# Routing of a token-choice mixture: compare and one-hot matrices by token column, idle products moved behind the first choice

## The chip, the cores and the metric

The kernel runs as one launch on one NeuronCore of a Trainium2 chip. The metric is the device time of that core in microseconds (us), the median of three runs. A core has a tensor engine (PE in the profile; its weight loads, the loads of the stationary operand, are listed apart as PEld), a vector engine (DVE), a scalar engine (ACT), a general engine (POOL) and a queue that issues transfers (SP). Each engine works through its own instructions in the order in which they were issued; engines wait for each other through semaphores.

## What is computed

Three layers, one after the other: attention with a compressive memory, a dense layer with a rational activation, and a mixture of experts. The change touches the last alone. Of the reference, cut:

```python
def _moe2_ref(x, w_gate, w1, w2):            # N = 2304 tokens, D = 512, E = 8 experts, F = 1024
    cap = N // E                             # 288
    order = np.argsort(-(x @ w_gate).flatten())
    for idx in order:
        tok, e = (int(idx) // E, int(idx) % E)
        if assigned[tok] >= 0 or counts[e] >= cap:
            continue
        assigned[tok] = e
        counts[e] += 1
...
    for e in range(E):
        mask = assigned == e
        out[mask] = np.maximum(x[mask] @ w1[e], 0.0) @ w2[e]
```

All pairs of token and expert are visited from the largest logit to the smallest; a pair is taken if the token is free and the expert has fewer than 288 tokens.

## The kernel before

**Two programs in a row.** `main` computes attention, the dense layer and the logits of all tokens (to about 869 us); `route` assigns the tokens and computes the experts (from there to the end). Nothing of `main` is changed.

**A choice.** `route` never sorts. In eight rounds (`phase(p)`, called a choice here) it finds which expert fills up next and which 288 tokens it gets. The logits lie as `Lt`, 128 partitions by 18 token columns by 8 experts. In a choice every free token stands for its best expert (`E1`, a one-hot over 8); the largest logit threshold at which some expert has 288 candidates is searched as an integer key of three digits, each by two passes of `search` (`st` = 45, then 1), so six passes. The last choice searches nothing. A pass is a ring between two engines:

- DVE compares 45 thresholds with each token's digit: `cm`, 810 elements of float16 on 128 partitions, laid out as 45 rows (thresholds) of 18 token columns;
- PE counts: 18 products, one for each token column c, whose stationary matrix is `cm[:, :, c]` (128 by 45; neighbours lie 18 elements, 36 bytes, apart) and whose moving matrix is `E1[:, c]` (8 columns), summed into `cnt` in PSUM;
- DVE flags what reaches 288 (`fl`) and sums the flags; PE adds them over the thresholds onto all partitions with one product by `one`; DVE takes `st` times that sum from the digit (`r`). After every second pass three small DVE operations (`dh`, `da`, `r`) bring in the next digit.

Behind the passes a choice computes the expert's number `ei`, the members (`GE`, counted by products with `one` and `tri`), their positions (`pos`), and turns positions to token numbers: `OH`, a one-hot over 32 (576 elements as 32 rows of 18 columns), is the stationary operand of 18 more products with `pay`; their sum is copied (`pls`) and made into three lists of 96 token numbers (`ids`, `id`).

**An expert.** `gather` fetches the 288 rows by three indirect transfers that POOL issues (`yg`), `px` transposes them on PE, ACT and DVE split them into two float16 parts (`x`). `prep` loads the expert's weights (`rawa`, `rawb`; 4 MB together), which ACT and DVE split into `hia`, `loa`, `hib`, `lob`. `ffn` then multiplies: 96 products into `ph`, 96 into `po`, each with 288 moving columns, for the last expert 288 with 96. ACT and DVE empty `ph` (`hh`, `hl`); `send` transposes back and scatters rows to `out`.

**The order.** No instruction order is written by hand. Every operation is recorded, and `plan` makes a list schedule: an engine takes the operation of smallest priority number (`S.now`) among those that are ready by its table of costs. Choices are recorded at -1.0, expert p at about p, so the choices of later experts are drawn in between the products of earlier ones. The instructions are then issued in that order on every engine; all of them carry line 408 in the profile, and groups are told apart by tile names. Where `plan` sees PE wait ahead of the first product into a fresh float32 bank (`o.fresh`), it puts idle products of `idh` (128 columns, into the same place, read by nobody) in front; they are meant to keep the tensor engine's clock up.

Of the kernel before, what the change touches and what calls it, by code (L numbers as in the profile page):

```python
# [27 lines left out]
CAP = N // E  # L28
NC_ = N // 128
XS = 1024.0          # scale of x before its split  # L30
WS = 256.0           # scale of w_in, w_out before their split
DS = 1024.0          # scale of dg and of the gate's deviations
# [8 lines left out]
class View:  # L41
    """a tile or a part of one, made in the program when it is used"""
# [43 lines left out]
    def region(self):  # L86
        """the partitions and the bytes in them that the view covers"""
        if self.a is None:
            return 0, 1 << 30, 0, 1 << 30
        pb = self.t.pbytes  # L90
        o = self.a.__array_interface__["data"][0] - DUMMY.ctypes.data
        p, lo = divmod(o, pb)
        ends = [s * (n - 1) for s, n in zip(self.a.strides[1:], self.a.shape[1:])]
        hi = lo + self.a.itemsize + sum(x for x in ends if x > 0)
        return p, p + self.a.shape[0], lo + sum(x for x in ends if x < 0), hi


class Late:
    """an operand made when it is used, from parts of tiles and the result of an operation"""
# [8 lines left out]
class LTile(View):  # L108
# [9 lines left out]
    def reset(self, S):  # L118
        """a tile that an earlier schedule made"""
# [11 lines left out]
class Group:  # L131
    """tiles of equal room that the schedule hands out to whoever needs one first"""
# [42 lines left out]
class Sched:  # L175
# [16 lines left out]
    def record(self, eng, name, args, kw):  # L192
# [25 lines left out]
        o.fresh = None          # room in its bank that nothing has been written to  # L218
        if eng == "tensor" and w[0].t.dt == F32:
# [19 lines left out]
        if eng == "tensor":             # the groups of a bank one after the other  # L239
# [17 lines left out]
    def plan(self):  # L257
        """start times by a list schedule: an engine takes the first of its operations that are ready"""
# [10 lines left out]
        hold = {}          # operations that wait for a tile's slot or a pool  # L269
# [8 lines left out]
        def grant(tag, t):  # L278
            """the tag's next tiles take the slots that are free"""
# [28 lines left out]
        while done < len(ops):  # L308
# [37 lines left out]
            if e == "tensor":           # its clock is halved after a window of little work  # L346
# [3 lines left out]
                if o.fresh is not None:  # L350
                    # while it waits, products to the same place that nobody reads keep the clock up
# [16 lines left out]
            if o.lat < 0:           # a transfer: the queue is free, the data come later  # L368
                dma[0] = max(dma[0], end + (0.65 if o.name != "dma_start_transpose" else 0.1)) - o.lat
                fin = dma[0] + 0.9  # L370
                if o.name == "indirect_dma_start" and o.kw["in_offset"] is None:     # the next waits for it
# [52 lines left out]
SLACK = 1.6, 1.3     # for the two schedules  # L424
HW, HN = 3.41333, 3050     # the window of the tensor engine's clock, and the columns that keep it fast
# [11 lines left out]
def cost(o, w, r):  # L437
    """what the operation holds its engine for, in us"""
# [70 lines left out]
def main(S, q, k, v, M_prev, z_prev, beta, w_in, w_out, moe_a, moe_b, w_gate):  # L509
# [25 lines left out]
    # identity and index constants  # L535
# [21 lines left out]
    # the attention of the later batches beside the blocks of tokens that are ready  # L557
# [16 lines left out]
GB = [None]          # banks of PSUM  # L574
LIM = dict(s=3, loc=2, y=2, m=4)    # how many a kind may hold
TS = 3.2
TAIL = 6             # first block of the MLP with no attention beside it
# [3 lines left out]
EARLY = 4            # units of attention that run before the MLP  # L581
# [3 lines left out]
L1E = 0.0            # the same for the last block  # L585
GA = 0.3             # how much more urgent the gate of the last but one tokens is
# [5 lines left out]
XR = 2, 2            # parts of x kept  # L592
# [6 lines left out]
U_ATT = 14           # steps of a unit of attention  # L599
MS = 8               # steps of a block of the MLP  # L600


def merge(S, streams):
    """draw n steps from each stream, spread over its span; a stream's lead makes it more urgent"""
# [16 lines left out]
def params(nc, consts, beta, moe_a, moe_b):  # L621
    """the small parameters, broadcast to every partition"""
# [7 lines left out]
    # exp(-beta) - 1 from t = -beta / 64: a short series, then m -> m (m + 2) six times  # L630
# [21 lines left out]
    # the numerator of dg = g - g0, by DS: h (a1 + (a2 - g0 |b1|) h + a3 h^2) - g0 |b0| |h|  # L652
# [13 lines left out]
def attention(nc, ac, wk, ps, xb, X, G0, P0, q, k, v, M_prev, z_prev):  # L666
# [6 lines left out]
    # causal masks of the diagonal blocks, added by the tensor engine  # L673
# [9 lines left out]
    # tiles whose padding is set once  # L683
    V1, PH, MZ, QR = [], [], [], []
    for i in range(2):
# [4 lines left out]
        t = ac.tile([128, 2, 130], F16, name=f"mz_{i}")         # the memory, split, and beside it zeros  # L690
# [3 lines left out]
    # the parts of a unit, in chunks of 128 tokens: the last 64 on partitions 64.. of the last chunk  # L694
# [13 lines left out]
    def phi(p, c0, c1):  # L708
        """PS (elu(q) + 1), split"""
# [11 lines left out]
    def split(p, n, w):  # L721
        """AS p in two parts"""
# [5 lines left out]
    def turn(a, w, how):  # L728
        """AS a in two parts, with the keys on partitions"""
        t = wk.tile([128, 1024], F16, name="at", bufs=TB)  # L730
        a = a[:, 0:w]
        if how == 3:        # by the tensor engine
# [8 lines left out]
        if how == 2:        # the lower part on GpSimd  # L741
# [12 lines left out]
    def qk(u):  # L754
# [22 lines left out]
        # q and k with features on partitions, split  # L777
        g = wk.tile([128, 4, S], F16, name="qkg", bufs=1)       # high parts of q and k, low parts of k and q
# [16 lines left out]
        # for a head: q over its low parts, k likewise, and k with the parts swapped  # L795
# [9 lines left out]
    def memory(u):  # L805
        """the part of the memory, with its norm"""
# [980 lines left out]
```

## Time and profile before

| | us |
|---|---|
| median of 3 runs | 1239.42 (1238.64 to 1240.16) |
| span of the profiled execution | 1236.9 |
| busy in it: PE / DVE / ACT / POOL | 1020.0 / 1006.7 / 690.1 / 629.6 |
| first compare products of the first choice | at 872.2 |
| first products of the first expert | at 909.9 |
| last products of the last expert (`po`) | from 1228.49 |

The profile is one execution, recorded instruction by instruction. A "busy" column is the time in which an engine ran at least one instruction; a row `x18` in a timeline merges 18 instructions that follow each other. For a tile's rows three durations are given, min/median/max in ns. `PEclk` is the granted clock of the tensor engine as a share of 2.4 GHz; its other level, 1.2 GHz, is 0.50. An entry `[0.20 <-DVE E]` is idle time of the engine ahead of the row, and what ended it.

### The profile page before, as it was taken

The page shows a single profiled execution, that of the slowest core. Times are in us where ns is not written, and L with a number is a line of the kernel's source. Part 1 is how long each engine was busy: PE and PEld are TensorE (multiplying, and loading weights), DVE is VectorE, ACT ScalarE, POOL GpSimd, SP SyncE. Part 2 cuts the span into 40 slices and gives each one's busy share as a digit, 9 for nine tenths or more (in the row PEclk, how much of TensorE's full clock was granted, in tenths as well). Part 3 has the DMA queues.
Part 4 walks back from the last instruction along what each step waited for, and adds up shares of the span by engine and source line. Part 5 has one row for each costly group of instructions (what it writes and reads, how often), then busy time and mean ns, then how long its engine had stood idle before and what let it go on. Part 6 is the DMA issues. An engine that isn't in the chain of part 4 may idle for free. (4 is left out here: it accounts for less than half of the span.)

```text
span 1236.9 us, 28684 instructions
## 1 busy us (share of the span) xinstructions
PE 1020.0 (82%) x11140; PEld 751.2 (61%) x11140; DVE 1006.7 (81%) x2309; ACT 690.1 (56%) x1443; POOL 629.6 (51%) x549
## 2 busy tenths in 40 slices
PE   4567877777788887887988989985789989999997
PEld 3445544354455655565665766663677767777776
DVE  7999999999999898999898989898466655766531
ACT  5776766546666776676775655650044434444542
POOL 3466578885766566656756556562031423334311
PEclk8688888987999998899999999996569988998999
DMA  8766564124565465555454211120044343543521
GB/s 212 211 155 144 114 138 119 22 27 69 138 106 109 96 121 108 106 100 106 86 91 70 53 19 35 32 65 10 1 156 156 108 143 101 175 145 129 165 87 40
DMA packets 220415, 125.77 MB, mean 102 GB/s; under 512 B 190870, under 2 KB 197110, under 8 KB 220152
## 3 DMA queue, kind: packets, MB, share of 16 engines
q1 hardware_dynamic: 217208, 114.51, 39.1%
q0 software_dynamic: 3072, 9.44, 2.6%
q8 instruction: 87, 1.43, 0.5%
q14 instruction: 48, 0.39, 0.1%
HBM read 71.96 MB, written 9.46 MB: 66 GB/s over the span
## 5 line engine op out<-in xcount | busy, mean ns | idle before, releaser
L408 PE MATMUL b<-W2h,dg 128*128 128x512 f16 x576 | 194.7, 393 | 15.2 <-POOL dg L408 8.0
L408 DVE TENSOR_TENSOR_SCAN yd<-A,b 128x256 f32<-128x256 f32 x272 | 165.5, 663 | 10.3 <-PE b L408 10.3
L408 PE MATMUL b<-X,W1h 128*128 128x64 f16 (+3 forms) x2432 | 168.5, 220 | 0.0
L408 POOL TENSOR_TENSOR nm<-nm,dn 128x512 f32<-128x512 f32 x72 | 98.4, 1368 | 95.9 <-ACT dn L408 51.4
L408 PEld LDWEIGHTS <-W1h 128*128 128x128 f16 x2432 | 137.2, 99 | 7.9 <-issue 2.5
L408 PEld LDWEIGHTS <-dg 128*128 128x128 f16 x864 | 80.1, 100 | 96.0 <-issue 16.5
L408 ACT ACTIVATE a<-b,mx 128x512 f32<-128x512 f32 (+4 forms) x160 | 78.5, 521 | 84.9 <-DVE b L408 59.9
L408 POOL TENSOR_TENSOR dn<-dn,u 128x512 f32<-128x512 f32 x72 | 98.8, 1374 | 43.4 <-ACT dn L408 41.7
L408 POOL TENSOR_TENSOR dg<-nm,dg 128x512 f16<-128x512 f32 x72 | 90.6, 1261 | 44.1 <-ACT dg L408 43.9
L408 PE MATMUL b<-W2l,dg 128*128 128x512 f16 x288 | 112.8, 392 | 0.0
L408 ACT ACTIVATE dn<-dn 128x512 f32<-128x512 f32 x144 | 90.1, 628 | 33.3 <-POOL dn L408 32.1
L408 PE MATMUL b<-X,W1l 128*128 128x64 f16 (+3 forms) x1216 | 98.6, 222 | 6.4 <-DVE yd L408 3.3
L408 PE MATMUL b<-qk 128*128 128x128 f16 (+5 forms) x384 | 75.8, 328 | 20.7 <-DVE at L408 9.6
L408 PE MATMUL ph<-x,hia 128*128 128x288 f16 x512 | 88.2, 306 | 0.0
L408 PEld LDWEIGHTS <-W1l 128*128 128x128 f16 x1216 | 73.2, 100 | 19.0 <-issue 6.0
L408 PE MATMUL b<-Wd,gT 99*128 99x64 f16 x1088 | 51.4, 199 | 40.1 <-DVE yd L408 12.0
L408 POOL DMA_INDIRECT yg<-Yd,id x24 | 33.8, 1408 | 97.6 <-ACT hia L408 41.0
L408 PE MATMUL b<-vh,at 128*128 128x65 f16 (+1 forms) x768 | 61.4, 205 | 25.7 <-DVE yd L408 5.2
L408 PEld LDWEIGHTS <-at 128*128 128x128 f16 x1152 | 54.1, 102 | 46.6 <-issue 29.9
L408 PEld LDWEIGHTS <-cm 128*45 128x45 f16 x756 | 68.0, 182 | 22.0 <-DVE E L408 7.6
L408 PEld LDWEIGHTS <-gT 99*128 99x128 f16 x1088 | 44.2, 102 | 60.8 <-DVE yd L408 20.7
L408 DVE TENSOR_SCALAR_CACHE_REDUCE b<-b 128x512 f32<-128x512 f32 (+4 forms) x160 | 75.7, 487 | 6.5 <-PE b L408 5.9
(250 smaller groups left out, 2716.5 us busy)
## 6 DMA issues: line engine op xcount, KB each, us to landing
rawa<-moe_w SPq DMA_DIRECT2D x32, 512.0 KB, 3.8
rawb<-moe_w SPq DMA_DIRECT2D x32, 512.0 KB, 4.0
qk<-qkg SPq DMA_DIRECT2D x64, 216.0 KB, 3.6
raw<-moe_w_in SPq DMA_DIRECT2D x16, 512.0 KB, 4.9
raw<-moe_w_out SPq DMA_DIRECT2D x16, 512.0 KB, 6.6
Yd<-yt SPq DMA_DIRECT2D x17, 256.0 KB, 2.0
qkr<-k SPq DMA_DIRECT2D x32, 128.0 KB, 2.5
qkr<-q SPq DMA_DIRECT2D x32, 128.0 KB, 3.2
```

Source lines behind the costliest of these rows:

```text
L408: o.ins = f(*[real(x) for x in o.args], **{k: real(x) for k, x in o.kw.items()})
```

## The change

- `cm` and `OH` keep their contents but are stored by token column: 18 columns of 45 thresholds, 18 columns of 32 positions. The tables they are compared with (`kst`, `io32`) are laid out alike. A stationary matrix `cm[:, c, :]` or `OH[:, c, :]` is now 45 or 32 neighbouring elements. In the comparison the token's value is repeated along the innermost dimension (step 0), where before it was read along it (step 1).
- The product that sums the flags has a stationary matrix of -45 or -1 (`less`) in place of ones, so that `r` is one addition; two memsets make the matrices, two signs turn in the expert's number.
- `plan` no longer puts idle products in front of `cnt` products (the condition on the name `cnt`).
- In the first choice 12 products of `idh` with 512 columns of `OH` are recorded behind the `OH` products, into a bank of `px`.

The diff without its hunks that only drop comments:

```diff
-        if eng == "tensor" and w[0].t.dt == F32:
+        if eng == "tensor" and w[0].t.dt == F32 and w[0].t.name != "cnt":
             o.fresh = w[0] if w[0].t.wr else w[0].t[:, 0:128]
...
-    kst = {st: iota([128, KT, C], [[st, KT], [0, C]], st if st == 1 else st + 1, 0, f"kst{st}", F16) for st in (KT, 1)}
-    io32 = iota([128, 32, C], [[1, 32], [0, C]], 1, 0, "io32", F16)
+    kst = {st: iota([128, C, KT], [[0, C], [st, KT]], st if st == 1 else st + 1, 0, f"kst{st}", F16) for st in (KT, 1)}
+    io32 = iota([128, C, 32], [[0, C], [1, 32]], 1, 0, "io32", F16)
...
+    less = {}
+    for st in (KT, 1):
+        less[st] = rc.tile([KT, 128], F16, name=f"less{st}")
+        nc.vector.memset(less[st], -float(st))
...
-            cm = rk.tile([128, KT, C], F16, name="cm")
-            nc.vector.tensor_tensor(cm, kst[st], r[:, None, :].to_broadcast([128, KT, C]), OP.is_le)
+            cm = rk.tile([128, C, KT], F16, name="cm")
+            nc.vector.tensor_tensor(cm, kst[st], r[:, :, None].to_broadcast([128, C, KT]), OP.is_le)
...
-                nc.tensor.matmul(pc[0:KT, 0:E], cm[:, :, c], E1[:, c, :], start=c == 0, stop=c == C - 1)
+                nc.tensor.matmul(pc[0:KT, 0:E], cm[:, c, :], E1[:, c, :], start=c == 0, stop=c == C - 1)
...
-            nc.tensor.matmul(pb[:, 0:1 + E], one[0:KT, :], fl, start=True, stop=True)
+            nc.tensor.matmul(pb[:, 0:1 + E], less[st], fl, start=True, stop=True)
...
-            nc.vector.scalar_tensor_tensor(r2, pb[:, 0:1].to_broadcast([128, C]), -float(st), r, op0=OP.mult, op1=OP.add)
+            nc.vector.tensor_scalar(r2, r, pb[:, 0:1], None, op0=OP.add)
...
-            nc.vector.scalar_tensor_tensor(fe, pb[:, 1:1 + E], -16.0, em8, op0=OP.mult, op1=OP.add)
+            nc.vector.scalar_tensor_tensor(fe, pb[:, 1:1 + E], 16.0, em8, op0=OP.mult, op1=OP.add)
...
-            nc.vector.scalar_tensor_tensor(me, pb[:, 0:1], 16.0, mf, op0=OP.mult, op1=OP.add)
+            nc.vector.scalar_tensor_tensor(me, pb[:, 0:1], -16.0, mf, op0=OP.mult, op1=OP.add)
...
-        OH = rk.tile([128, 32, C], F16, name="OH")
-        nc.vector.tensor_tensor(OH, io32, posh[:, None, :].to_broadcast([128, 32, C]), OP.is_equal)
+        OH = rk.tile([128, C, 32], F16, name="OH")
+        nc.vector.tensor_tensor(OH, io32, posh[:, :, None].to_broadcast([128, C, 32]), OP.is_equal)
...
-            nc.tensor.matmul(pl[0:32, 0:18], OH[:, :, c], pay[:, c].rearrange("p a j -> p (a j)"), start=c == 0, stop=c == C - 1)
+            nc.tensor.matmul(pl[0:32, 0:18], OH[:, c, :], pay[:, c].rearrange("p a j -> p (a j)"), start=c == 0, stop=c == C - 1)
+        if p == 0:
+            up = ps.tile([128, 512], F32, name="px", bufs=2)
+            for _ in range(WARM):
+                nc.tensor.matmul(up, G0["idh"], OH.rearrange("p c k -> p (c k)")[:, 0:512], start=True, stop=True)
...
+WARM = 12
```

The change also moves instructions, since `plan` works with other costs. PE, first choice, between the first and the second pass, before (`E_13306` is `E1`; 7 idle products ahead of the flag product, 12 behind it; in the whole program 146 idle products into `cnt`):

```order
L408 LDWEIGHTS cm
L408 MATMUL cnt<-E_13306,cm 45x8
L408 LDWEIGHTS idh
L408 MATMUL cnt<-idh 128x128
...
L408 LDWEIGHTS one
L408 MATMUL cnt<-fl,one 128x9
L408 LDWEIGHTS idh
L408 MATMUL cnt<-idh 128x128
...
L408 LDWEIGHTS cm
L408 MATMUL cnt<-E_13306,cm 45x8
```

The same place now (`less_13269` is the matrix of -45):

```order
L408 LDWEIGHTS cm
L408 MATMUL cnt<-E_13309,cm 45x8
L408 LDWEIGHTS less_13269
L408 MATMUL cnt<-fl,less_13269 128x9
L408 LDWEIGHTS cm
L408 MATMUL cnt<-E_13309,cm 45x8
```

Between the passes of the first choice PE now issues nothing but the ring's own products.

PE at the end of the first choice now; where before 6 idle products into `cnt` stood ahead of the `OH` products and 5 behind, 12 into `px` and 2 of the new 512-column products stand ahead and 10 behind:

```order
L408 MATMUL cnt<-GE,tri 128x36
L408 LDWEIGHTS idh
L408 MATMUL px<-idh 128x128
...
L408 LDWEIGHTS idh
L408 MATMUL px<-OH,idh 128x512
...
L408 LDWEIGHTS OH
L408 MATMUL cnt<-pay,OH 32x18
...
L408 LDWEIGHTS idh
L408 MATMUL px<-OH,idh 128x512
```

The 10 behind stand ahead of the first compare products of the second choice.

DVE behind the first choice, a piece of the difference (`pls` to `id` make the lists that the first gather waits for; `loa` is the low part of a piece of the first expert's weights):

```order
+L408 TENSOR_TENSOR cm<-kst_13256,kf_13602 128x810
 L408 COPY pls<-cnt 32x18
+L408 SCALAR_TENSOR_TENSOR loa<-rawa,hia 128x512
 L408 SCALAR_TENSOR_TENSOR ids<-pls 32x3 x3
-L408 COPY id_13726<-ids 96x1
-L408 COPY id_13729<-ids 96x1
-L408 COPY id_13733<-ids 96x1
+L408 SCALAR_TENSOR_TENSOR loa<-rawa,hia 128x512
+L408 COPY id_13647<-ids 96x1
+L408 COPY id_13649<-ids 96x1
+L408 COPY id_13652<-ids 96x1
```

Two weight pieces that stood behind the three lists now stand between their steps.

## Rows read from the trace of the kernel before

**Rows 1.** The page: the span.

```profile
span 1236.9 us, 28684 instructions
```

**Rows 2.** Busy time by stretch: PE, PEld, DVE, ACT, POOL, then PEclk, DMA.

```profile
900.50:939.20 38.70, 36.70 (x296) 28.67 (x295) 24.25 (x104) 17.66 (x37) 10.67 (x9) 0.74 0.43 150
939.20:978.10 38.90, 38.48 (x321) 30.31 (x321) 23.04 (x99) 18.29 (x38) 13.07 (x12) 0.91 0.42 144
978.10:1021.30 43.20, 38.66 (x315) 30.30 (x314) 26.95 (x102) 17.92 (x39) 12.96 (x12) 0.86 0.34 117
1021.30:1060.00 38.70, 37.76 (x316) 29.34 (x315) 24.33 (x95) 16.46 (x37) 11.53 (x10) 0.89 0.37 120
1060.00:1098.40 38.40, 37.05 (x323) 29.42 (x322) 25.82 (x100) 18.56 (x40) 13.83 (x12) 0.96 0.41 141
1098.40:1142.60 44.20, 41.73 (x353) 32.79 (x353) 27.32 (x111) 20.99 (x46) 16.49 (x15) 0.92 0.41 142
1142.60:1229.00 86.40, 81.76 (x869) 68.71 (x869) 33.35 (x72) 37.01 (x83) 20.97 (x15) 1.00 0.32 107
```

**Rows 3.** DVE's waits, 924 to 1144 us: total, times, longest.

```profile
DVE fl L408 <- PE cnt L408: 48.9, 31, 2.9
DVE r L408 <- PE cnt L408: 19.8, 23, 2.2
```

**Rows 4.** Tile cm: durations in ns, min/median/max.

```profile
L408 PEld LDWEIGHTS <-cm x756: 158/183/186, 872.2 to 1130.6; 128*45 128x45 f16 x189
L408 DVE TENSOR_TENSOR cm<-kst,r x35: 567/582/2795, 875.1 to 1127.9; 128x810 f16<-128x810 f16 x35
```

**Rows 5.** Tile OH: durations in ns.

```profile
L408 PEld LDWEIGHTS <-OH x144: 135/159/163, 898.0 to 1143.6; 128*32 128x32 f16 x144
L408 DVE TENSOR_TENSOR OH<-io,posh x8: 449/450/453, 897.5 to 1141.1; 128x576 f16<-128x576 f16 x8
```

**Rows 6.** A load of neighbouring columns (by form); 16 short products in a row (timeline).

```profile
L408 PEld LDWEIGHTS <-qk 128*64 128x64 f16 x128 | 6.7, 115 | 19.3 <-issue 9.7 <-DVE at L408 6.3 <-DVE yd L408 1.3
...
470.05 0.63 PE L408 MATMUL b<-Wd,gT 99*128 99x64 f16 x16 [0.15 <-DVE qkg L408]
470.51 0.95 PE L408 MATMUL b<-X,W1h 128*128 128x64 f16 x14
```

**Rows 7.** Timeline of the first choice: its start, its third pass, its end.

```profile
872.16 1.71 PE L408 MATMUL cnt<-E,cm 128*45 128x8 f16 x18 [7.40 <-DVE E L408]
...
880.29 1.71 PE L408 MATMUL cnt<-E,cm 128*45 128x8 f16 x18
881.93 0.93 PE L408 MATMUL cnt<-idh 128*128 128x128 f16 x7
882.03 0.17 DVE L408 TENSOR_SCALAR_CACHE_REDUCE fl<-cnt 45x8 f16<-45x8 f32 x1 [2.06 <-PE cnt L408]
882.79 0.18 PE L408 MATMUL cnt<-fl,one 45*128 45x9 f16 x1
883.01 0.18 DVE L408 SCALAR_TENSOR_TENSOR r<-cnt,r 128x18 f16<-128x18 f32 x1 [0.81 <-PE cnt L408]
883.22 0.58 DVE L408 TENSOR_TENSOR cm<-kst,r 128x810 f16<-128x810 f16 x1
884.30 1.71 PE L408 MATMUL cnt<-E,cm 128*45 128x8 f16 x18
...
894.88 0.19 PE L408 MATMUL cnt<-GE,one 128*128 128x36 f16 x1 [0.30 <-DVE GE L408]
```

**Rows 8.** Timeline between the first choice and the first expert.

```profile
898.65 1.23 PE L408 MATMUL cnt<-pay,OH 128*32 128x18 f16 x18 [2.91 <-DVE pay L408]
900.37 0.16 DVE L408 COPY pls<-cnt 32x18 f32<-32x18 f32 x1
902.19 1.46 POOL L408 DMA_INDIRECT yg<-Yd,id  x1 [40.98 <-ACT hia L408]
909.95 1.17 PE L408 MATMUL ph<-x,loa 128*128 128x288 f16 x4
```

## Prediction

> **What bounds the kernel now.** I read three views. The busy time by stretch comes first, cut where each choice has its first compare products [rows 2]. From 900.5 to 1142.6 us PE is busy 230.4 of 242.1 us, and in the last stretch 81.8 of 86.4, while DVE has work for 151.7 of the 242.1. So PE sets the pace behind the first choice, and a choice period is some 40 us. The granted clock there is 0.74 to 0.96: as a mix of the two levels (1.2 and 2.4 GHz) that makes (1 - 0.74)/0.5 x 38.7 = 20 us at the lower level in the first of these stretches and 7, 12, 8, 3 and 7 in the next ones, 58 together. The second view is DVE's waits [rows 3]: from 924 to 1144 it stands 48.9 + 19.8 = 69 us for counts that PE has not made yet. Slack of DVE is there, and it lies exactly at the ring between DVE and PE. The third is the timeline of the first choice [rows 7], 872.2 to 894.9, when nothing else runs: there the ring itself is the path, DVE and PE in turn.
>
> **What the counting products cost, before and after.** A pass holds PE from 880.29 to 881.93, 1.64 us for 18 products, 91 ns each [rows 7], though 8 columns move. What holds it is the load: 45 columns 36 bytes apart take 183 ns, 32 such columns 159 [rows 4, 5]; that is (183 - 159)/13 = 1.8 ns a column. A load of 64 neighbouring columns takes 115 ns [rows 6], less than either. A strided load lasts 92 ns beyond its spacing (183 - 91); with the same 92 to 95, 64 neighbours stream in 20 to 23 ns, 45 of them in some 15, and at the lower clock I take twice that and more, 30 to 40. So after the change the load is no longer the limit at the upper level; the shortest spacing that the trace shows is the next row: 16 products with 64 columns start within 470.05 to 470.51, 29 ns each [rows 6]. I take 29 ns at the upper level (18 x 29 = 0.52 us and 0.02 to turn, 0.54) and 38 at the lower (0.68). The ends are 25 and 55.
>
> [...]
>
> **Comparisons.** [...] I take 1.00, so +0.42 a comparison and +0.30 an `OH`. The other end is no change (0). [...]
>
> **First choice, on the path.** A pass without a new digit takes 4.01 us (880.29 to 884.30). Its pieces [rows 7]: 1.64 + 0.10 to `fl`; 0.17 to its end; then the flag product at 882.79, 0.59 after that end although 0.06 would do, because idle products stand in front of it; 0.22 to `r`; 0.21 to `cm`; 0.58; and 0.50 until the products start at 884.30, again behind idle products, where 0.05 would do (872.16 shows a start right on the data). After: 0.68 + 0.10 + 0.17 + 0.06 + 0.22 + 0.21 + 1.00 + 0.05 = 2.49, and 0.1 for the last product's way into PSUM, which the slower loads hid; 2.6. The passes with a new digit have 0.49 more for `dh`, `da`, `r`. From 872.16 to the `GE` product at 894.88 are 22.7 us; three passes at 2.6, two at 3.1 and a last one, whose `r` leads to `GE` and not to a comparison, of some 2.5 give 16.5. Ahead of them the first comparison and two memsets delay `E1` by 0.45. So -5.8; ends -4.5 and -6.5.
>
> **From there to the first expert.** From 894.88 to 909.95 are 15.1 us [rows 7, 8]. `OH` is ahead of `pay`: +0.3. Two of the 512-column products stand ahead of the `OH` products, 0.43 each at the lower level, and wait for `OH`, as `pay` also takes about 0.7 more: +0.15. The 18 products start from 898.65 in 1.23 us; with neighbouring columns they take 0.6: -0.6. The second choice's comparison ahead of `pls` (900.37): +0.4. Two `loa`, which need the first weight pieces, now stand ahead of the lists: 0.7 each, and the first must wait for its piece: +1.5 or so, and the first gather (902.19) waits for the lists. Together +1.8; ends 0 and +2.5. The 10 idle products behind take 10 x 0.43 = 4.3 us of PE, about 894 to 898 on the new clock; the gathered rows come 8 us after the lists, so PE is free in time, and what they hide behind is that gather. If it were gone they would cost 4.3. Net of both parts -4.0.
>
> **The long stretch.** 42 passes less six of the first choice leave 36. About two of them run while the first rows are fetched; 34 x (1.64 - 0.54) = 37.4 us of PE. The `OH` products of seven choices save 7 x 0.6 = 4.2. Both come off an engine that is busy 95% of the time, so I count them whole: -41.6. DVE gets 34 x 0.42 + 7 x 0.30 = 16 us more; 151.7 + 16 over 242 - 41 is 84%, and the waits of 69 us [rows 3], which shrink with each faster count, hide it. If that cover is gone, part of the 16 us is paid. The idle products into `cnt` behind 900.5 are few, and what replaces them is as much; `r` and the signs are the same number of DVE instructions. POOL and SP issue the same transfers.
>
> **Sum.** The profiled execution has a span of 1236.9 [rows 1], 2.5 us under the median of 1239.4; I keep that distance. 1236.9 - 4.0 - 41.6 + 2.5 = 1193.8, say **1194 us**, with PE's lost time (idle, and at the lower clock) unchanged.
>
> **Rivals.**
> - *The ring becomes the bound.* DVE at 84%, in order, with 0.7 us weight pieces between the ring's steps, no longer keeps up, and a pass is worth only 1.10 - 0.42 = 0.68. For: the ring runs choice after choice without a break, and DVE does 25 us or so of work per period. Against: the 69 us of waits. Long stretch 34 x 0.68 + 7 x 0.3 = 25 instead of 42: 1211.
> - *The clock rises.* A compare pass moves 8 columns in 1.64 us, and stretches with such passes show the lower level. With the passes a third as long, and the 512-column products in front of the first expert, half of the 58 us could go to the upper level: half of 29 saved, 15: 1179. Against: in the first expert PE waits for transfers, and nothing in the rows says the upper level is held there.
> - *The layout does nothing for the load* (slower). Load time would go by the count when it is not 128, not by the stride; 64 columns at 115 ns speak against it [rows 6]. Then the passes stay at 1.64, the comparison's 0.42 lies on the ring, 34 x 0.42 + 7 x 0.3 = 16, and the first choice gains at most 5 x 0.98 from the idle products (0.53 and 0.45 in the pass shown), less 5 x 0.42, 0.45 and the 1.8 behind: about even. 1255. It decides from a spacing of 91 - 420/18 = 68 ns upwards.
> - *The comparison keeps its speed.* First choice another 2.5 lower, DVE relieved: 1190, inside the forecast's own range.
>
> **How the numbers follow.** Forecast 0.55 (1184 to 1204), the ring 0.20 (1204 to 1217), the clock 0.14 (1172 to 1184), comparison as before 0.05, layout or a disturbed order that costs time 0.05, no change 0.01. Range 1176 to 1214: it leaves out the slow case, the ends of ring and clock, under 0.2. Faster by over 0.2% (about what a measurement of this kernel can tell from no change): 0.94; within 0.2%: 0.01; slower: 0.05.
>
> **What would show it.** Loads of `cm` near 100 ns in place of 183; 18 products in 0.5 to 0.7 us; `cm` near 1.0 us; the `GE` product of the first choice near 889; first expert's products near 906; choice periods near 34 us with PE above 90% busy and DVE's waits for `cnt` far below 69 us. Wrong if periods stay above 37 us with PE idle in front of counts (ring), if PEclk in these stretches is at 1.0 (clock), or if loads stay at 183.

## The result, and the profile after

The changed kernel takes 1203.4 us (median of 4 runs, 1200.7 to 1205.9) where the kernel before takes 1239.0 on the same chip: a ratio of 0.9725, 95% interval 0.9694 to 0.9757. It is faster by 35.6 us; forecast were 45, with 1176 to 1214 as the range. The page of the changed kernel, its span and its engines:

```profile
span 1203.0 us, 28471 instructions
...
PE 963.6 (80%) x11029; PEld 694.7 (58%) x11039; DVE 1033.0 (86%) x2311; ACT 691.4 (57%) x1443; POOL 631.0 (52%) x549
```

PE has 56 us less work than before (1020.0), DVE 26 us more (1006.7). The stretches between the first compare products of the choices, as [rows 2] has them for before (PE, PEld, DVE, ACT, POOL, then PEclk, DMA share, GB/s):

```profile
902.20:935.90 33.70, 28.73 (x299) 21.26 (x298) 24.37 (x95) 16.25 (x36) 11.87 (x9) 0.84 0.43 144
935.90:975.90 40.00, 31.88 (x302) 22.94 (x302) 27.34 (x99) 16.73 (x37) 17.15 (x12) 0.83 0.40 134
975.90:1012.90 37.00, 34.27 (x352) 25.52 (x353) 28.14 (x103) 20.35 (x44) 13.23 (x11) 0.95 0.40 136
1012.90:1050.00 37.10, 31.24 (x324) 22.77 (x325) 30.26 (x102) 19.01 (x41) 14.72 (x12) 0.95 0.46 153
1050.00:1083.80 33.80, 30.37 (x337) 23.30 (x338) 29.65 (x101) 18.05 (x40) 13.27 (x11) 1.00 0.43 142
1083.80:1120.10 36.30, 33.35 (x358) 24.96 (x359) 31.55 (x112) 20.62 (x45) 17.27 (x16) 1.00 0.52 177
1120.10:1195.10 75.00, 73.15 (x805) 61.33 (x804) 32.02 (x69) 33.32 (x75) 15.42 (x13) 1.00 0.37 120
```

Before, PE was busy 95% of these stretches up to the last one; now 190 of 218 us, 87%. The granted clock is higher (0.93 as a mean against 0.88). The loads and the comparison after, to be laid beside [rows 4, 5]:

```profile
L408 PEld LDWEIGHTS <-cm x756: 98/100/136, 875.9 to 1105.7; 128*45 128x45 f16 x189
...
L408 DVE TENSOR_TENSOR cm<-kst,r x35: 985/1003/3743, 877.6 to 1103.5; 128x810 f16<-128x810 f16 x35
...
L408 PEld LDWEIGHTS <-OH x144: 92/93/113, 897.2 to 1120.5; 128*32 128x32 f16 x144
```

A load fell from 183 to 100 ns, the comparison rose from 582 to 1003.

**Where the 34 us of the profiled executions lie.** I cut both traces at the same events: the choice's first operation (`v`), the first `GE` product, the first product of the first expert, the last product of the last.

| us | before | changed | forecast |
|---|---|---|---|
| start to `v` (code unchanged) | 869.1 | 872.5 (+3.4) | 0 |
| `v` to the `GE` product | 25.76 | 20.37 (-5.4) | -5.8 |
| `GE` to the first expert | 15.07 | 17.05 (+2.0) | +1.8 |
| long stretch | 318.84 | 284.98 (-33.9) | -41.6 |
| tail | 8.15 | 8.10 | 0 |

The part ahead of `v` scatters: in the 14 profiles of this case it ends between 868.4 and 876.4 with the same code. So the table of the experiments gives the length from `v` to the end, the *route*, beside the times: 367.8 us before, 330.5 now. All columns of that table behind the ratio are read from one profiled execution each, and those of `cnt2` (1239.1 us), `rstt` (1210.1) and `slack` (1253.3, one of two long runs that its time and ratio leave out) lie 6 us and more above their kernel's median, that of `pair` (1201.9) 8 below it.

**The long stretch taken apart.** The whole stretch, then what of PE works on `cm` and on `ph`, before:

```profile
909.95:1228.80 318.85, 303.06 (x2709) 241.62 (x2708) 178.69 (x657) 140.87 (x302) 93.78 (x79) 0.92 0.37 127
909.95:1228.80 318.85, 58.03 (x612) 55.07 (x612) 23.46 (x34) 0.92 0.37 127
909.95:1228.80 318.85, 121.19 (x770) 28.71 (x64) 26.12 (x64) 0.92 0.37 127
```

and the same three of the changed kernel:

```profile
909.90:1194.90 285.00, 257.81 (x2700) 197.68 (x2698) 199.25 (x654) 140.83 (x301) 97.18 (x78) 0.95 0.43 142
909.90:1194.90 285.00, 21.65 (x612) 18.63 (x612) 40.42 (x34) 0.95 0.43 142
909.90:1194.90 285.00, 111.71 (x772) 28.64 (x64) 26.05 (x64) 0.95 0.43 142
```

PE's work fell by 303.06 - 257.81 = 45.2 us, more than the 41.6 forecast: 36.4 less on `cm`, 4.6 on `OH` (8.86 to 4.26) and 9.5 on `ph`, but 5.2 more on `po` (109.22 to 112.79) and `px` (28.78 to 30.38). The `ph` part is mostly clock: of the experts' products with 288 columns, those that start some 240 ns after the one before them (the lower level) instead of 122 fell from 124 to 62, within `ph` from 98 to 33. (288 columns in 240 ns, at a granted clock of 0.50, are 1.2 columns a ns; in 122 ns, at 1.00, some 2.4: these are the two levels that are called 1.2 and 2.4 GHz.) But PE's idle time in the stretch rose from 15.8 to 27.2. What PE waits for there, before:

```profile
PE cnt L408 <- DVE pay L408: 3.2, 2, 3.0
PE cnt L408 <- DVE cm L408: 2.8, 4, 1.4
...
PE ph L408 <- DVE hl L408: 2.5, 3, 1.5
```

and now:

```profile
PE cnt L408 <- DVE cm L408: 9.5, 7, 3.1
PE px L408 <- DMA yg<-Yd,id: 4.9, 5, 2.2
PE cnt L408 <- DVE GE L408: 2.6, 2, 1.7
```

The wait for the comparison is new. With the waits that the profile puts down to the operation issued just ahead of the counts (`id`, `e`), PE stands 12.5 us in front of counting products, 3.7 before.

**What a late comparison looks like.** The longest of those waits, PE, DVE and POOL together:

```profile
957.78 1.14 PE L408 MATMUL ph<-x,hia 128*128 128x288 f16 x8
...
958.41 5.28 POOL L408 TENSOR_TENSOR lob<-rawb,hib 128x512 f16<-128x512 f32 x4 [1.25 <-ACT rawb L408]
958.62 1.84 DVE L408 TENSOR_TENSOR cm<-kst,r 128x810 f16<-128x810 f16 x1
960.52 0.61 PE L408 MATMUL cnt<-E,cm 128*45 128x8 f16 x18 [1.59 <-DVE cm L408]
...
961.60 1.02 DVE L408 TENSOR_SCALAR r<-r,cnt 128x18 f16<-128x18 f16 x1 [0.26 <-PE cnt L408]
962.65 1.90 DVE L408 TENSOR_TENSOR cm<-kst,r 128x810 f16<-128x810 f16 x1
...
964.61 0.56 PE L408 MATMUL cnt<-E,cm 128*45 128x8 f16 x10 [3.06 <-DVE cm L408]
```

While POOL makes four low parts (1.32 us each), both comparisons take 1.84 and 1.90 in place of 1.00, and the addition that makes `r` takes 1.02 in place of 0.24. Counted behind the first expert's start: 6 additions and 6 comparisons last more than 0.25 us beyond the median, all 12 overlap a `TENSOR_TENSOR` of POOL, and their excess is 6.2 and 6.9 us. Before, 4 comparisons did (3.6 us), and no addition; over all operations of DVE this excess is some 17 us against 11. The rows of the two forms of `r`, first before:

```profile
L408 DVE SCALAR_TENSOR_TENSOR r<-cnt,r x30: 157/176/179, 909.2 to 1132.0; 128x18 f16<-128x18 f32 x30
```

and in the changed kernel:

```profile
L408 DVE TENSOR_SCALAR r<-r,cnt x29: 224/243/2434, 913.4 to 1107.0; 128x18 f16<-128x18 f16 x29
```

What waits differs by form: the new `r`, one tensor and a value for each partition, takes 243 ns and up to 2434; `cm`, two tensors in SBUF, is stretched before (582, up to 2795) and after (1003, up to 3743); the old `r`, with its second tensor in PSUM, never takes more than 179. The new `r` ends 0.03 to 0.04 us behind the low part that holds it, in each of the six cases; where low parts follow each other at once it can wait for two of them, as in the case of 2434 ns.

**Theory.** The layout did what was forecast to PE's work. The gain that is missing is PE idle time: DVE's part of the ring became longer, by the comparison's 0.42 us and by an addition that has to wait for POOL, and it is no longer covered. *Rivals*: the gain is not the layout's but that of the moved idle products; the idle time comes from the order alone (counts placed too early by `plan`); the lists or gathered rows are what is late.

### The profile page after: what moved, and what is told of

It reads as the page before. It is cut to its first block, busy times and chain, and to the rows that moved or that the text cites. A ratio compares the mean times of both kernels' runs of the same rounds, so it can differ in the third digit from the quotient of the medians.

```text
span 1203.0 us, 28471 instructions
## 1 busy us (share of the span) xinstructions
PE 963.6 (80%) x11029; PEld 694.7 (58%) x11039; DVE 1033.0 (86%) x2311; ACT 691.4 (57%) x1443; POOL 631.0 (52%) x549
## 4 chain that ended last, share of the span: by engine, by line
DVE 36%; PE 22%; issue 8%; DMA 6%; ACT 5%; POOL 2%; SPq 0%; POOLq 0%; DVEq 0%; ACTq 0%
PE b L408 9%; DVE yd L408 7%; DVE nm L408 7%; PE po L408 5%; PE ph L408 4%; DVE nat L408 3%; DVE A L408 3%; PE cnt L408 2%; DVE cm L408 2%; DVE b L408 2%; DMA gT<-gm 1%; DVE loa L408 1%; ACT a L408 1%; PE px L408 1%; DMA rawb<-moe_w 1%
## 5 line engine op out<-in xcount | busy, mean ns | idle before, releaser
L408 PEld LDWEIGHTS <-dg 128*128 128x128 f16 x864 | 80.4, 101 | 96.9 <-issue 17.8
L408 PE MATMUL b<-qk 128*128 128x128 f16 (+5 forms) x384 | 79.4, 341 | 19.9 <-DVE at L408 9.0
L408 PE MATMUL b<-vh,at 128*128 128x65 f16 (+1 forms) x768 | 63.9, 209 | 28.6 <-DMA at<-nat 6.4
L408 PE MATMUL b<-Wd,gT 99*128 99x64 f16 x1088 | 51.3, 198 | 41.1 <-DMA gT<-gm 10.1
L408 PE MATMUL ph<-x,hia 128*128 128x288 f16 x512 | 80.8, 293 | 0.0
L408 DVE SCALAR_TENSOR_TENSOR nm<-u,pr,nm 128x512 f32<-128x512 f32 x72 | 76.6, 1064 | 0.7
L408 POOL DMA_INDIRECT out<-ot,id x24 | 26.3, 1098 | 96.4 <-ACT ot L408 70.1
```

Source lines behind the costliest of these rows:

```text
L408: o.ins = f(*[real(x) for x in o.args], **{k: real(x) for k, x in o.kw.items()})
```

## The experiments

All in one table; ratios are to the kernel before, on the same chip. "Low" is the number of 288-column products at the lower level. `again` is the changed kernel measured once more, beside `rstt`, `pairrstt` and `pool0`; 1201 to 1206 us was expected of it.

| kernel | median us (range) | ratio (95%) | route | `v` to `GE` | `GE` to expert | stretch | PE idle in it | low |
|---|---|---|---|---|---|---|---|---|
| before | 1239.0 | 1 | 367.8 | 25.8 | 15.1 | 318.8 | 15.8 | 124 |
| changed | 1203.4 (1200.7 to 1205.9) | 0.9725 (0.969, 0.976) | 330.5 | 20.4 | 17.1 | 285.0 | 27.2 | 62 |
| again | 1205.0 (1204.8 to 1210.9) | 0.9755 (0.971, 0.980) | 329.7 | 20.4 | 16.5 | 284.7 | 28.1 | 60 |
| layout | 1218.8 (1217.8 to 1220.6) | 0.9822 (0.977, 0.988) | 343.7 | 23.3 | 17.1 | 294.4 | 32.1 | 83 |
| idle | 1240.9 (1235.6 to 1246.4) | 1.0007 (0.998, 1.004) | 365.7 | 22.4 | 18.4 | 316.8 | 15.1 | 122 |
| warm0 | 1207.7 (1205.8 to 1210.1) | 0.9755 (0.971, 0.980) | 332.1 | 20.4 | 17.1 | 286.5 | 29.9 | 57 |
| cmp2 | 1243.0 (1240.2 to 1248.0) | 1.0038 (1.001, 1.007) | 365.0 | 26.6 | 19.6 | 310.7 | 48.1 | 97 |
| cnt2 | 1231.0 (1227.8 to 1239.1) | 0.9952 (0.993, 0.998) | 363.1 | 24.7 | 17.5 | 312.7 | 31.4 | 122 |
| pair | 1209.7 (1201.9 to 1211.4) | 0.9756 (0.970, 0.981) | 326.6 | 18.1 | 16.1 | 283.4 | 27.1 | 75 |
| pairsame | 1198.2 (1197.4 to 1201.4) | 0.9680 (0.964, 0.972) | 323.8 | 18.0 | 16.7 | 281.1 | 25.2 | 59 |
| rstt | 1203.9 (1198.9 to 1210.1) | 0.9725 (0.968, 0.977) | 331.8 | 20.0 | 16.5 | 287.2 | 25.7 | 89 |
| pairrstt | 1193.1 (1191.6 to 1197.0) | 0.9657 (0.961, 0.970) | 321.3 | 17.7 | 17.6 | 278.0 | 21.7 | 58 |
| pool0 | 1230.4 (1227.3 to 1234.9) | 0.9943 (0.991, 0.997) | 354.3 | 20.4 | 16.6 | 309.2 | 43.7 | 102 |
| slack | 1239.6 (1233.0 to 1247.5) | 1.0001 (0.997, 1.004) | 376.7 | 20.5 | 17.0 | 331.1 | 47.5 | 155 |

### Which part of the change carries the gain: layout, idle, warm0

`layout` is the changed kernel with the two moves of idle products undone:

```diff
-        if eng == "tensor" and w[0].t.dt == F32 and w[0].t.name != "cnt":
+        if eng == "tensor" and w[0].t.dt == F32:
...
-        if p == 0:
+        if p == 0 and WARM:
...
-WARM = 12
+WARM = 0
```

> The new layout of cm and OH alone: idle products into cnt are put in front as before, and the 12 products of 512 columns are not issued. If the layout carries the gain: PE is free of some 0.8 to 1.0 us in each of 34 later passes, and a pass of the first choice gets 1.64 - 0.8 shorter and its comparison 0.42 longer: 1202 to 1208 us, first choice (v to the GE product) some 24 us, passes as in the changed kernel. If the move of the idle products carries a good part of it through the clock: 1215 us or more, with more products of the experts at the lower clock than the 62 of the changed kernel.

`idle` makes the same two moves alone in the kernel before:

```diff
-        if eng == "tensor" and w[0].t.dt == F32:
+        if eng == "tensor" and w[0].t.dt == F32 and w[0].t.name != "cnt":
...
+        if p == 0:
+            up = ps.tile([128, 512], F32, name="px", bufs=2)
+            for _ in range(WARM):
+                nc.tensor.matmul(up, G0["idh"], OH.rearrange("p k c -> p (k c)")[:, 0:512], start=True, stop=True)
...
+WARM = 12
```

> The layout of before; only the idle products into cnt are gone and the 12 products of 512 columns stand behind the first choice. If only waits between the passes of the first choice go: 5 x (0.53 + 0.45) = 4.9 us in the first choice, nothing behind it: 1233 to 1236 us. If the idle products' place is worth more through the clock: the count of expert products at the lower clock falls from 124 by 50 or so, 0.12 us each: 1228 us or less. If PE loses its clock by their absence: 1239 or more.

`warm0` is the changed kernel with `WARM = 0`, so that only the 12 products go:

> The changed kernel without the 12 products of 512 columns behind the first choice; idle products into cnt stay away. If the 12 lie hidden beside the first gather and do nothing for the clock: 1201 to 1205 us. If they carry the upper level into the first expert: more of its products at the lower clock than 62 and 1206 to 1211 us. If it is their absence that makes the kernel with the new layout alone 15 us slower than the changed one: 1215 us or more; else that is the idle products ahead of cnt in the long stretch.

`layout` alone gives 20.6 of the 35.6 us, less than I expected. It is the time of the second case, with its sign: 83 products at the lower level in place of 62, which makes some 2.5 us. `idle` alone gives nothing: the first choice gets 3.4 us shorter and the way to the first expert 3.4 longer. Its time is that of the third case, but a loss of clock is not to be seen (122 products, 124 before), so that the idle products into `cnt` keep the clock up is not shown. The 12 products are not told apart from nothing (0.9725 or 0.9755 with them, 0.9755 without), and the way from `GE` to the first expert is the same without them, 17.1: they lie hidden there, as the prediction said. They don't carry the upper level into the first expert either, since without them 57 products are at the lower one.

What remains between `layout` and `warm0`, 11 us by the medians, is the idle products in front of `cnt`. The two differ in the first choice by 2.9 us and in the stretch by 7.9: 61 idle products into `cnt` take 5.1 us of PE there (11 and 1.9 us in the kernel before, none in `warm0`), and the longest operations differ as well (10 additions stretched, 15.0 us in all, against 6.2 in the changed kernel), since the order is another one. So the move is worth something only together with the new layout, with which `plan` would put more idle products in front of the counts than before. How the 11 us divide among its parts stays open.

### The price of a us on each engine of the ring: cmp2, cnt2

`cmp2` issues each comparison twice in place, `cnt2` each counting product (with the threshold at twice the count):

```diff
                 o.ins = f(*[real(x) for x in o.args], **{k: real(x) for k, x in o.kw.items()})
+                if o.name == "tensor_tensor" and o.args[0].t.name == "cm":
+                    o.ins = f(*[real(x) for x in o.args], **{k: real(x) for k, x in o.kw.items()})
```

> The changed kernel with each comparison issued twice in the same place: 42 x 1.00 us more for DVE, the result and the order otherwise the same. If DVE's waits still cover its work behind the first choice: 6 us from the first choice alone, 1209 us. If the ring is the bound there: 42 us, 1245 us. My theory that PE's added idle time is a part of DVE's added time coming to the surface lies between: 6 + about half of 36, 1227 us, with PE's idle time in the long stretch (27 us now) up by the same.

```diff
-                o.ins = f(*[real(x) for x in o.args], **{k: real(x) for k, x in o.kw.items()})
+                kw = {k: real(x) for k, x in o.kw.items()}
+                if o.name == "matmul" and o.eng == "tensor" and o.args[1].t.name == "cm":
+                    f(*[real(x) for x in o.args], **{**kw, "stop": False})
+                    kw["start"] = False
+                o.ins = f(*[real(x) for x in o.args], **kw)
...
-            nc.vector.tensor_scalar(fl[:, 1:], pc[0:KT, 0:E], CAP - 0.5, 0.0, op0=OP.is_ge, op1=OP.max, accum_out=fl[:, 0:1])
+            nc.vector.tensor_scalar(fl[:, 1:], pc[0:KT, 0:E], 2 * CAP - 0.5, 0.0, op0=OP.is_ge, op1=OP.max, accum_out=fl[:, 0:1])
```

> The changed kernel with each of the 18 counting products issued twice (the threshold doubled, the result the same): 18 x 26 ns = 0.47 us more PE per pass at the upper level, 0.74 at the lower. If a us of counting counts whole, as the prediction's sum has it: 36 x 0.5 + 6 x 0.7 = 22 us, 1225 us. If PE's idle time in front of counts takes part of it (the counts come later, the next comparison too, so the ring does not give room): still 1220 or more. If the long stretch has slack on PE: 1207 to 1212 us.

`cmp2`: the first choice is 6.2 us longer, as expected, and the long stretch 25.7, between my middle (18) and the ring (36); the time, 1243.0, is near the ring's 1245. DVE's time on `cm` in the stretch rises by 33.8 (40.42 to 74.18), so a us added to the comparison costs 0.76: 20.9 us of the 25.7 are idle time of PE, 4.8 are longer `ph` with 97 products at the lower level. Little cover is left above its present length.

`cnt2`: PE's time on `cm` rises by 17.8 (21.65 to 39.46) and the stretch by 27.8, the whole of it and more. The rest is 8.0 us on `ph` (111.71 to 119.75) and 4.2 of idle time, less some on `po` and `px`: 122 instead of 62 of the experts' products are at the lower level, as before the change. By the medians the kernel is 27.6 us slower than the changed one, of which 4.3 belong to the first choice, so some 23 us are left for the stretch, still more than 17.8. So a us of counting counts whole, as the prediction's sum has it, and the clock comes on top. The clock's part of the gain is gone where the time in counting products is put back. Counting is not all that moves it: `cmp2` counts as the changed kernel does and has 97 products at the lower level, with 48 us of idle time.

### Taking the comparison's 0.42 us back: pair, pairsame

`pair` keeps the new layout but stores each digit twice side by side (46 thresholds in place of 45), so that the operand of the comparison has step 1 along its innermost two elements; `OH` likewise:

```diff
-            cm = rk.tile([128, C, KT], F16, name="cm")
-            nc.vector.tensor_tensor(cm, kst[st], r[:, :, None].to_broadcast([128, C, KT]), OP.is_le)
+            cm = rk.tile([128, C, KT], F16, name="cm")
+            two = lambda x: x.rearrange("p c (k t) -> p c k t", t=2)
+            nc.vector.tensor_tensor(two(cm), two(kst[st]), r[:, :, None, :].to_broadcast([128, C, KT // 2, 2]), OP.is_le)
```

> The changed kernel with every digit stored twice side by side, 46 thresholds in place of 45, and the comparison reading the value as a pair (innermost step 1), OH likewise: the load stays contiguous. If step 0 is what halves DVE's rate, cm takes 0.58 us in place of 1.00 and OH 0.45 in place of 0.75: first choice 2.5 us shorter, and if a part of the comparison's time is what stands behind PE's idle time, the long stretch 5 to 12 us shorter: 1188 to 1196 us. If PE's idle time has other causes (transfers, lists): 1200 us. If a fourth dimension of the access costs DVE its rate: cm at 1.0 us and 1203 us.

Its comparison takes 0.59 us and the first choice is 2.3 shorter, but the time, 1209.7, lies above all three forecasts. `plan` sees the shorter costs and makes another order. The trace, 8 us under the median and with a route 3.9 us shorter than the changed kernel's, shows longer waits of PE for `pay` (6.2 us in place of 2.0) and `cm` (11.5 in place of 9.5), but not why the median is higher. `pairsame` sets the costs in the planner so that every engine has the changed kernel's order:

> The kernel with paired digits, its costs in the planner set so that every engine has the changed kernel's order; only durations differ: cm 0.58 in place of 1.00, OH 0.45 in place of 0.75. The doubled comparison cost some 0.7 us of the long stretch for each us of DVE; at that price 36 x 0.42 x 0.7 = 11 us and 2.5 in the first choice: 1190 us. If the ring only binds at some passes and a shorter comparison just waits for what comes next in the fixed order: 2.5 us and 3 or so, 1197 to 1200 us. If the first paired kernel's order was not its trouble: 1203 to 1210 us.

1198.2, and no run of it (to 1201.4) reaches one of `pair` (from 1201.9), so the order was `pair`'s trouble. First choice 2.4 shorter, long stretch 3.9, the outcome of a ring that binds only at some passes. DVE's busy time there fell by 14.0 us (199.25 to 185.24), so a us taken off the comparison brings 0.28, where one put on costs 0.76. Of the 16 us that the prediction lets DVE's waits hide, about 4 were not hidden.

### The wait for POOL: rstt, pairrstt, pool0

`rstt` writes the addition as two tensors, one in PSUM, in the unchanged order:

```diff
-            nc.vector.tensor_scalar(r2, r, pb[:, 0:1], None, op0=OP.add)
+            nc.vector.scalar_tensor_tensor(r2, pb[:, 0:1].to_broadcast([128, C]), 1.0, r, op0=OP.mult, op1=OP.add)
```

> The changed kernel with the addition that makes r written again as the operation of before (two tensors, one from PSUM) in place of a tensor plus a value for each partition; every engine keeps its order. In the trace of the changed kernel 6 of 34 additions stretch from 0.24 to 1.0 to 1.6 us, 6.2 us in all, each while POOL makes a low part; in before none of the old form did. If the new form has to wait for POOL and that wait lies in the open: the long ones vanish and the time falls by 4 to 6, to 1198 us. If POOL's pieces then stretch the comparisons behind them instead, or the waits are covered: 1201 to 1205 us.

The additions of `rstt` (min/median/max in ns):

```profile
L408 DVE SCALAR_TENSOR_TENSOR r<-cnt,r x29: 157/177/179, 916.4 to 1112.6; 128x18 f16<-128x18 f32 x29
```

What PE waits for in its long stretch (912.9 to 1200.1):

```profile
PE px L408 <- DMA yg<-Yd,id: 10.1, 4, 4.4
PE cnt L408 <- DVE cm L408: 4.8, 5, 1.9
PE cnt L408 <- DVE GE L408: 2.6, 2, 1.6
```

Not one addition is stretched any more, and PE's wait for `cm` fell from 9.5 to 4.8. But its wait for the gathered rows rose from 4.9 to 10.1, and the time is the changed kernel's (1203.9 beside 1205.0), as the second case has it. That the old form of `r` takes these waits away is shown; that they cost time by themselves is not: in this trace, what PE wins in front of the counts it waits for in front of `px`.

`pairrstt` has both, paired digits and this addition, in the changed kernel's order:

> Paired digits in the changed kernel's order, and r by the operation of before: both reliefs of DVE's part of the ring at once. If they add: 1198 less the 5.2 us by which additions stretch there, 1193 us. If the waits only move on to the comparison: 1196 to 1199 us.

What PE waits for in its long stretch (903.6 to 1181.6):

```profile
PE px L408 <- DMA yg<-Yd,id: 7.8, 4, 3.8
PE cnt L408 <- DVE GE L408: 3.0, 3, 1.7
PE cnt L408 <- DVE cm L408: 2.9, 3, 1.5
```

In front of `cm` PE waits 2.9 us, as before the change (2.8). 1193.1 us, and no run of it (to 1197.0) reaches one of the changed kernel beside it (from 1204.8): some 12 us faster, the best of the kernels here. Route -8.4, of it 2.7 in the first choice and 6.7 in the stretch, less 1.1 on the way to the first expert. In these two profiles another 5.2 lie ahead of `v`, where nothing differs. The time is the one expected if both reliefs add; but against `pairsame` the route is only 2.5 us shorter and the intervals of the two ratios overlap, so what the addition's form is worth by itself stays open.

`pool0` gives POOL's low parts to DVE:

```diff
-    PL = {"a": (6, 7), "b": (4, 5, 6, 7)}, {"a": (), "b": ()}, {"a": (), "b": ()}
+    PL = [{"a": (), "b": ()}] * 3
```

> The changed kernel with POOL's 36 low parts made by DVE (0.68 us each, 24 us more for DVE; ACT is spared 36 scalings); the planner knows, so the order differs. If operations of DVE that wait for POOL are what PE's added idle time comes from: the 17.8 us of stretching are gone, and idle falls towards the 16 us of before: 1193 to 1199 us. If DVE's plain load matters more: 1206 us and up.

The comparison and the addition of `pool0` (min/median/max in ns):

```profile
L408 DVE TENSOR_TENSOR cm<-kst,r x29: 985/1003/1005, 910.5 to 1127.8; 128x810 f16<-128x810 f16 x29
L408 DVE TENSOR_SCALAR r<-r,cnt x29: 228/243/245, 914.6 to 1131.1; 128x18 f16<-128x18 f16 x29
```

Without `TENSOR_TENSOR` on POOL neither form is stretched once (maxima 1005 and 245 ns), which settles what they had waited for. The time went up to 1230.4 all the same, as the second case has it: PE's idle time is 43.7 us, 22.8 of it for gathered rows. It tells nothing on the price of the collisions, since 24 us of work moved to DVE and the order with it.

### The order: slack

`slack` plans with longer latencies between the engines:

```diff
+SLACK = SLACK[0], 2.2
```

> The changed kernel, planned with latencies between engines taken 2.2 times instead of 1.3, so that PE has more expert products in front of each step of the ring; only the order differs. If PE's 27 us of idle time come from counts placed before their comparison is done: idle falls by 10 or more and the time to 1190 to 1196 us. If the ring has no room (six passes, lists, gather and split must fit in a period of 34 us): the waits move to the lists and to px and ph, 1203 us or more.

It went as the rival has it: 1239.6. In its trace PE still waits 15.6 us for `cm`, and 17.3 for gathered rows. So this order, with more expert products planned in front of each step, doesn't help. It is not a test of the order alone: POOL's low parts fall otherwise, and six additions wait for them for 17.2 us in all (6.2 in the changed kernel). That the ring, the lists and the gather have to fit into a period that is now shorter is my reading, and not shown.

## Why the prediction was right, and where it was not

- *Loads and counting.* Right. The load is 100 ns (near 100 said), a row of 18 lasts 0.61 us at the upper level and 0.88 at the lower; start to start the products lie 26 ns apart at the upper level and 41 at the lower, 29 and 38 in the sum; at a stride of 36 bytes they lay 87 apart. The 38 was an estimate that no row of before shows. Of 37.4 us, 36.4 came. `OH` products: 4.6 for 4.2.
- *Comparisons.* Right: 1.003 us and 0.752 for 1.00 and 0.75. No row of before shows the 1.00 and the 0.75 that the sum takes. Between 576 and 810 elements the runs show (1003 - 752)/234 = 1.07 ns for each further element with step 0, and (582 - 450)/234 = 0.56 before, with step 1.
- *First choice.* Right: from the first compare products to the `GE` product 16.9 us, 16.5 worked out. The third pass, to be laid beside that in [rows 7], takes 2.69 us from start to start, 2.6 worked out and 4.01 before:

```profile
881.79 0.88 PE L408 MATMUL cnt<-E,cm 128*45 128x8 f16 x18 [1.86 <-DVE cm L408]
...
882.71 0.17 DVE L408 TENSOR_SCALAR_CACHE_REDUCE fl<-cnt 45x8 f16<-45x8 f32 x1 [0.98 <-PE cnt L408]
...
882.94 0.16 PE L408 MATMUL cnt<-fl,less 45*128 45x9 f16 x1 [0.26 <-DVE fl L408]
883.14 0.24 DVE L408 TENSOR_SCALAR r<-r,cnt 128x18 f16<-128x18 f16 x1 [0.26 <-PE cnt L408]
883.41 1.00 DVE L408 TENSOR_TENSOR cm<-kst,r 128x810 f16<-128x810 f16 x1
...
884.48 0.88 PE L408 MATMUL cnt<-E,cm 128*45 128x8 f16 x18 [1.38 <-DVE cm L408]
```

- *From `GE` to the first expert.* Right: +2.0 for +1.8, and for the reason given. The lists are done behind the low parts; the changed kernel's timeline there:

```profile
898.16 0.99 DVE L408 TENSOR_TENSOR cm<-kst,kf 128x810 f16<-128x810 f16 x1
...
899.07 0.16 DVE L408 COPY pls<-cnt 32x18 f32<-32x18 f32 x1
899.16 0.67 DVE L408 SCALAR_TENSOR_TENSOR loa<-rawa,hia 128x512 f16<-128x512 f32 x1
...
900.88 0.26 DVE L408 COPY id<-ids 96x1 int32<-96x1 int32 x3
...
901.99 1.35 POOL L408 DMA_INDIRECT yg<-Yd,id  x1 [38.21 <-DMA rawa<-moe_w]
```

From `pls` to that gather are 2.9 us, 1.8 before, and from the `GE` product 9.1, 7.3 before [rows 7, 8]. The row puts the gather's wait down to a transfer of `rawa`, but in all 14 traces the first gather starts 0.84 to 0.85 us behind the third list, whatever is named there.

- *The long stretch.* The term that was mis-sized: -41.6 forecast, -33.9 measured. The failing step is "with PE's lost time (idle, and at the lower clock) unchanged". PE's lost time changed twice, in opposite directions: the clock gave back some 62 x 0.118 = 7.3 us on the experts' products, and idle time took 11.4. With all its parts PE's work fell by 45.2, 3.6 more than forecast, and 11.4 less 3.6 is the miss. The prediction's rivals of the ring and of the clock both came true in part. By the sum that gave 58 us at the lower level before, 32 are left, near the half that the clock's rival names, but the 7.3 are only half of its price. That the miss stayed this small is partly luck: without the 7.3 us of clock the time would have been near 1211, where the ring's rival stands and close to the end of the range.
- *Why the idle time rose.* The step that names the cover, 69 us of DVE waiting for counts, took an average for a guarantee. DVE's waits for counts did shrink, to 29 us, to be laid beside [rows 3] (909.9 to 1120):

```profile
DVE fl L408 <- PE cnt L408: 15.1, 17, 1.5
DVE r L408 <- PE cnt L408: 13.7, 16, 1.8
```

But they are not gone, and PE waits for `cm` all the same. A pass that PE held for 1.64 us had also hidden most late comparisons (PE waited 2.8 us for `cm`), since PE arrived late itself; at 0.6 it arrives on time and sees them. That is a reading of the waits, which the runs bear out in part: the comparison's 0.42 is some 4 us of it (`pairsame`). "`r` and the signs are the same number of DVE instructions" was right as a count and wrong as a price: the new form waits for POOL, 6 times in 34, and with the old one PE waits less in front of the counts (`rstt`: 9.5 to 4.8). In `pairrstt` PE's wait for `cm` is back at that of before, and the longest that remains is for the rows of the gather (7.8).
- *Idle products.* "The idle products into `cnt` behind 900.5 are few" was right of the kernel before (11 in the long stretch); with the new layout alone there are 61 (`layout`). So their removal, which the sum puts at nothing there, belongs to what the change gained.
- *What would show it.* Of the six periods two are near the 34 us named (33.7 and 33.8), the others 36.3 to 40.0, and PE is below 90% in four. Periods above 37 with PE idle in front of counts were named as the mark of the ring; 40.0 and 37.1 are such. The `GE` product (892.85) and the first expert's products (909.9) came 3.9 us later than named, 3.4 of it ahead of `v`.

Left open: how the 11 us between `layout` and `warm0` divide, what the addition's wait for POOL costs by itself, why `po` and `px` take 5.2 us more of PE, and what scatters the part ahead of `v` by up to 8 us.

## What to carry to other kernels

When a step on the bounding engine gets shorter, price first what had been late behind it: the waits of the other engine show its mean slack, not whether each of its operations came in time. An operation that is rewritten in another form is a change to its price even where the count of instructions stays (176 ns became 243 here); on DVE look whether the new form waits for what POOL does at that moment (up to 2434 ns in the changed kernel, and 179 at most in the old form). Where an operand that is repeated with step 0 makes a comparison slower, try storing the value twice, which keeps the layout (591 ns for 828 elements in place of 1003 for 810 here), and if a planner orders the code, compare with the order held fixed.

## What the runs showed of the hardware that I had not expected

A stationary matrix of 45 neighbouring columns can be loaded and used every 26 ns at the upper level and every 41 at the lower one; the same 45 at a stride of 36 bytes take 87 in all 42 passes before, 12 of them wholly at a granted clock of 0.50 and 28 at 1.00. Values stored in pairs and read with step 1 over two elements restore the rate of before (582 ns for 810), as the comparison of `pairrstt` shows (828 elements; 1003 ns for 810 with step 0):

```profile
L408 DVE TENSOR_TENSOR cm<-kst,r x35: 571/591/3329, 873.0 to 1088.8; 128x828 f16<-128x828 f16 x35
```

And an addition of 18 elements, written as a tensor and a value for each partition, takes up to 2434 ns in the changed kernel where POOL makes low parts beside it (243 as the median, 245 at most in `pool0`, where POOL makes none), and 179 at most in the form of two tensors, one of them in PSUM (before and `rstt`).
